# GpSimd copies two thirds of a shifted V tile, and the first column slot is kept in picture order

## The chip, the cores and the metric

The kernel runs on one core of a Trainium2 chip. A core has a matrix engine (TensorE, PE in the profile, with its weight loads as PEld), VectorE (DVE), ScalarE (ACT), GpSimd (POOL), and SyncE (SP), whose queue only issues transfers here. The metric is the device time of one launch in microseconds; lower is better.

## The reference, cut to what matters

The kernel computes neighborhood attention with 7x7 neighbours at a distance of 2 over a 224x224 picture of 192 channels:

```python
qkv = x @ wqkv                                  # x: (1, 224, 224, 192)
q, k, v = qkv[..., :C], qkv[..., C:2*C], qkv[..., 2*C:]
half = (7 - 1) // 2 * 2
r0 = clip(arange(H) - half, 0, H - 1 - 12)      # first row of the window
c0 = clip(arange(W) - half, 0, W - 1 - 12)      # first column of it
ri = r0[:, None] + arange(7) * 2
ci = c0[:, None] + arange(7) * 2
logits = einsum(q[n], k[rows ri, columns ci]) * C ** -0.5
o = einsum(softmax(logits), v[rows ri, columns ci]) @ wo
```

A pixel near the left edge has its window clipped to the start of the row. The pixels 0 to 5 of a row therefore look at the first window of even columns or at the first window of odd columns; on the right edge it is the same with the last windows.

## The kernel before

**Tiles.** With a distance of 2, a pixel only meets pixels of its own row and column parity. The kernel sorts the queries by the parity class of the rows (`rc`) and of the columns (`cc`) that they look at. The work goes in 14 steps: `steps` (L602) lists seven bands (`ti`) of 16 query rows, for both row classes. A step has 14 column slots of 8 query columns; slot 0 holds the clipped ones. A slot is a tile of 16 rows by 8 columns, 128 queries in all, once for each of the two column classes. Partitions 0 to 63 hold the first 8 rows and 64 to 127 the other 8.

**What is made for a step.** The input x is loaded transposed (L154, from SP) into XA and into a tile x1, of which GpSimd copies halves into XB (L160). GpSimd also sorts x by keys into XS (L170). From these TensorE makes two things.

- G is the query side with the key weights folded in: `g_items` (L395) multiplies x by AW. It works in four groups of slots, and each group is two whole tiles (`pg`, items g0 to g7) and one tile of halves (`pgh`, items h0 to h3). ACT evacuates them (L328); the halves go to a tile gx first, of which GpSimd copies each half into place (L450). `col_runs` (L378) says from which image columns the queries of a group come. It cuts them into runs that lie one behind the other in XA or XB; each run, for each run of rows, each half and both passes over the contraction, is one matmul at L415.
- V is the value side with wo folded in: `v_item` (L340), six matmuls (L335, L338) and one evacuation for each of 14 column blocks, items v0 to v13. The tile VV holds the values of the step. The second half of the queries reads it directly; the first half reads a tile in which the lower 64 partitions hold this step's values and the upper 64 those of the step before. `v_over` (L347) makes that tile: it copies partitions 0 to 63 from one VV tile to the other, in three pieces of column blocks. The pieces of the steps made in the background of steps 1 to 10 are blocks 0 to 4, 5 to 9 and 10 to 13, copied by DMAs that SP issues after items v4, v9 and v13 (L704 to L706). In the background of step 0 the pieces are 8, 3 and 3 blocks by DMAs that ACT (the first) and SP issue, and from the background of step 11 on they are 8, 3 and 3 blocks copied by GpSimd.

**What is done in a step.** A step is seven pairs of slots, and the loop at L714 runs over the 98 pairs. `stage1` multiplies G by x for the logits (L499) and takes the maximum with DVE (L501); `stage1b` takes the exponential with ACT (L508); `stage2` transposes the probabilities, by TensorE and a copy (L538, L539) or, for the pairs that TURN lists, by a DMA from SP (L522); `stage3` multiplies them by V (L548); `stage4` divides by the sum with DVE (L554, L571) and stores. stage3 runs two to three pairs behind stage1.

**Order.** All of it is written out by hand: the last call makes every engine run its instructions in program order. The items of the next step are mixed into the pairs by the tables BACK and LATE (steps 1 to 10, and later), with a lag of three pairs: item v9 is made in the first pair of the following step and v13 in its second, so the second and third piece of V's copy come there, and item h2 is made in the pair before them and h3 in the pair behind.

**Stores.** Slots 1 to 13 are stored by SP, in 96 KB for 16 rows, with a few short ones by GpSimd (L577). Slot 0 lies in another order: its columns are first three of one column parity and then those of the other, so that L597 lists five small stores for each run of rows in each half of a tile (L600). They are pushed into `pool_q` and issued by GpSimd, at most four items in a pair together with the sorts, which go ahead of them (L798, L804).

Of the kernel before, what the change touches and what calls it, by code (L numbers as in the profile page):

```python
# [19 lines left out]
S = 112  # L20
# [8 lines left out]
C = 192  # L29
# [38 lines left out]
def _win(t, p0, pn, off, dims):  # L68
    a = t[:]
    ps = a.ap[0][0]  # L70
    return bass.AP(a.tensor, a.offset + p0 * ps + off, [[ps, pn]] + [list(d) for d in dims])


def _x(par, v, c):

    return (v % RP) * RW + par * S + c
# [23 lines left out]
def kernel(  # L100
# [7 lines left out]
    nc = tc.nc  # L108
    B, H, W, C_ = x.shape
# [4 lines left out]
    op = out[0].rearrange("h (j two) c -> h j (two c)", two=2)  # L114
# [91 lines left out]
    for cc in range(2):  # L206
        t = pers.tile([128, S], BF, name=f"ch{cc}")
# [5 lines left out]
    d1 = setup.tile([128, MM], F32, name="d1")  # L213
# [133 lines left out]
    def v_over(rc, ti, c0, c1, eng=nc.sync.dma_start):  # L347

        eng(out=VV[rc][1 - ti % 2][0:64, c0:c1, :], in_=VV[rc][ti % 2][0:64, c0:c1, :])
# [26 lines left out]
        return runs  # L376

    def col_runs(cc, d0, d1):  # L378
        runs = []
        for d in range(d0, d1):  # L380
            if cc == 0:
                mem, pair = (1, d) if d < 3 else (0, d - 3)
            else:
                mem, pair = (1, 109 + d) if d < 3 else (0, 106 + d) if d < 6 else (1, d - 3)
            if runs and runs[-1][2] == mem and runs[-1][3] + runs[-1][1] == pair:
                runs[-1][1] += 1
            else:
                runs.append([d - d0, 1, mem, pair])
        return runs

    OUT_A = (0, 64)
# [3 lines left out]
    def g_items(rc, ti, s0, ns):  # L395
        rows = row_runs(rc, ti)
        w = 8 * ns

        def mm(pg, cc, p0, c0):

            out_ = []
            for (d0, dn, mem, pair) in col_runs(cc, 8 * s0, 8 * s0 + w):
                for (j, n, par, r) in rows:
                    o = _win(pg, p0, 64, j * w + d0, [[w, n], [1, dn]])
                    for pas in range(2):
                        X = (XA, XB)[pas][mem]
                        out_.append((o, AW[(mem, pas)][:, c0:c0 + 64], _win(X, 0, 128, _x(par, r, pair), [[RW, n], [1, dn]]), pas))
            return out_

        def both(a, b):  # L410
            for q in range(max(len(a), len(b))):
                for l_ in (a, b):
                    if q < len(l_):
                        (o, l, r, pas) = l_[q]
                        nc.tensor.matmul(o, lhsT=l, rhs=r, start=(pas == 0), stop=(pas == 1))  # L415

        def put(dst, off, pg, dve, p0=0, pn=128):

            a, m = s0, ns
            if s0 == 0:  # L420
                rr = [_runs8(rc, ti, h) for h in range(2)]
                if len(rr[0]) == len(rr[1]):
                    evac(_win(dst, p0, pn, off, [[64, 2], [8, 8], [1, 8]]), _win(pg, p0, pn, 0, [[8 * w, 2], [1, 8], [w, 8]]), dve)
                else:
                    for h in range(2):
                        for (j0, nj) in rr[h]:
                            evac(_win(dst, p0, pn, off + 64 * h + 8 * j0, [[nj, 8], [1, nj]]), _win(pg, p0, pn, (8 * h + j0) * w, [[1, 8], [w, nj]]), dve)
                a, m = 1, ns - 1
            evac(_win(dst, p0, pn, off + (a - s0) * 128, [[8, 16], [128, m], [1, 8]]), _win(pg, p0, pn, 8 * (a - s0), [[w, 16], [8, m], [1, 8]]), dve)

        def whole(cc):
            def emit(dve):
                pg = ps_g.tile([128, 512], F32, name="pg", tag="pg")
                both(mm(pg, cc, 0, OUT_A[cc]), mm(pg, cc, 64, OUT_A[cc] + 64))
                put(G[rc][cc], s0 * 128, pg, dve)
            return emit

        def halves(dve, direct=False):
            pg = ps_g.tile([128, 512], F32, name="pgh", tag="pg")
            pg1 = ps_o.tile([128, 512], F32, name="pgh", tag="o") if direct else pg  # L440
            both(mm(pg, 0, XDAT[0], OUT_B[0]), mm(pg1, 1, XDAT[1], OUT_B[1]))
            if direct:
                put(G[rc][0], (NSLOT + s0) * 128, pg, False, XDAT[0], 64)
                put(G[rc][1], (NSLOT + s0) * 128, pg1, True, XDAT[1], 64)
                return
            gx = work.tile([128, 512], BF, name="gx", tag="gx", bufs=3)
            put(gx, 0, pg, dve)
            for cc in range(2):
                p = XDAT[cc]
                nc.gpsimd.tensor_copy(out=G[rc][cc][p:p + 64, 1, s0:s0 + ns, :], in_=gx[p:p + 64, 0:ns * 128].rearrange("p (s q) -> p s q", q=128))  # L450

        return [whole(0), whole(1), halves]
# [104 lines left out]
    def stage4(J, ab):  # L557
        rc, ti, s, o_ps = J.rc, J.ti, 2 * J.m + ab, J.o_ps[ab]
        rs = J.rs.get(ab) or stage4a(J, ab)
        if s > 0 and J.n == NSTEP - 1:  # L560

            o_sb = _win(XS[0], 0, 128, 2 * C * s, [[C, 2], [1, C]])
        elif s > 0:
            o_sb = work.tile([128, 2, C], BF, name="o_sb", tag="o_sb", bufs=6)
        else:
            o_sb = work.tile([128, 2, C], BF, name="o_s0", tag="o_s0")
        if J.k >= NP - 3 and ab == 1:
            for cc in range(2):
                nc.scalar.mul(o_sb[:, cc, :], o_ps[:, 194 * cc:194 * cc + C], rs[:, cc:cc + 1])
        else:  # L570
            nc.vector.tensor_tensor(out=o_sb[:], in0=_win(o_ps, 0, 128, 0, [[194, 2], [1, C]]),  # L571
                                    in1=rs[:].unsqueeze(2).to_broadcast([128, 2, C]), op=ALU.mult)
        prow = _rows(rc, ti)
        if s > 0:
            for (j0, nj, r0, rstep) in _aff_runs(prow) if J.n < NSTEP - 1 else [(0, 12, prow[0], 2), (12, 1, prow[12], 1), (13, 3, prow[13], 2)]:
                def put(eng, j0=j0, nj=nj, r0=r0, rstep=rstep):
                    eng.dma_start(out=op[r0: r0 + (nj - 1) * rstep + 1: rstep, 8 * s - 3:8 * s + 5, :],  # L577
                                  in_=o_sb[8 * j0:8 * (j0 + nj)].rearrange("p t c -> p (t c)"))

                if J.n < NSTEP - 1:  # L580
                    put(nc.gpsimd if nj < 8 and s % 2 == 1 else nc.sync)
                elif nj >= 8:
                    put({NSLOT - 1: nc.scalar, NSLOT - 4: nc.gpsimd}.get(s, nc.sync))
                elif s in SHORT:

                    for j in range(nj):
                        def row(eng, p=8 * (j0 + j), r=r0 + j * rstep, a=SHORT[s]):
                            eng.dma_start(out=op[r, 8 * a - 3:8 * s + 5, :].rearrange("(t i) c -> i t c", i=8),
                                          in_=_win(XS[0], p, 8, 2 * C * a, [[2 * C, s + 1 - a], [1, 2 * C]]))
                        if s < NSLOT - 1:  # L590
                            row(nc.gpsimd)
                        else:
                            end_q.append(row)
            return
        for h in range(2):
            for (j0, nj, r0, rstep) in _aff_runs(prow[8 * h:8 * h + 8]):
                for (cc, i0, n, mem, pair) in ((0, 0, 3, 1, 0), (0, 3, 5, 0, 0), (1, 6, 2, 1, 3), (1, 0, 3, 1, 109), (1, 3, 3, 0, 109)):  # L597
                    p = 64 * h + 8 * j0 + i0 * nj
                    dst = op[r0: r0 + (nj - 1) * rstep + 1: rstep, pair:pair + n, mem * C:(mem + 1) * C]
                    pool_q.append(lambda dst=dst, p=p, m=n * nj, cc=cc: nc.gpsimd.dma_start(out=dst.rearrange("j i c -> i j c"), in_=o_sb[p:p + m, cc, :]))  # L600

    steps = [(ti, rc) for ti in range(7) for rc in range(2)]  # L602
    pairs = []
# [12 lines left out]
    act, dve, pool = nc.scalar.copy, nc.vector.tensor_copy, nc.gpsimd.tensor_copy  # L616
# [25 lines left out]
    pool_q = []  # L642
# [25 lines left out]
    t = ps_t.tile([128, 8, 128], BF, name="pt_ps", tag="pt")  # L668
# [33 lines left out]
    def back(it, by_dve):  # L702
        it(by_dve)
        for (i, c0, c1) in ((7, 0, 8), (10, 8, 11), (13, 11, 14)) if nb == 0 or nb >= 11 else ((4, 0, 5), (9, 5, 10), (13, 10, 14)):  # L704
            if it in vs and it is vs[i]:
                v_over(rcb, tib, c0, c1, pool if nb >= 11 else nc.sync.dma_start)  # L706

    def values_of(k):

# [4 lines left out]
    for k in range(NP + 2):  # L714
        J = pairs[k] if k < NP else None
        n = J.n if J else NSTEP
        w64, w128 = [], []
        if J:
            m = J.m
            nb, mb = divmod(k - LAG, 7)  # L720
            bg = k >= LAG and nb + 1 < NSTEP
            if bg and mb == 0:
                tib, rcb = steps[nb + 1]
# [115 lines left out]
```

## Time and profile before

| | before |
|---|---|
| median of 3 runs | 343.1 us (342.54 to 347.22) |
| the profiled execution's own time | 341.45 us |
| its span, first to last instruction | 339.7 us |
| TensorE busy | 322.4 us (95%), 7964 matmuls |
| VectorE busy | 311.0 us (92%) |
| ScalarE busy | 310.6 us (91%) |
| GpSimd busy | 288.2 us (85%) |
| packets on SP's DMA queue | 51.60 MB, 78.6% of 16 engines' span |
| small stores of slot 0 (L600) | 150, 84.5 us of GpSimd |
| SP's copies of V (L349) | 20 of 241.2 KB, 10 of 193.0 KB, 2 of 144.8 KB |

The busy times are for the whole span, and matmuls overlap, so a TensorE that is busy all the time is not yet one that is never held up. [...] A row of a group of instructions reads: line, engine, operation, what it writes and reads, shape of the output and the input, count, then busy time in us and mean ns of one, then the idle time of the engine ahead of them with what ended it. A wait that has several conditions is put down to the one that came last by the profile, which can be another than the one that decided.

### The profile page before, as it was taken

To read this page: it belongs to the slowest core of one execution; us is meant where nothing else is said; L and a number is where in the kernel's file an instruction comes from. 1 tells how busy PE (TensorE), PEld (TensorE's weight loads), DVE (VectorE), ACT (ScalarE), POOL (GpSimd) and SP (SyncE) were. 2 spreads that over 40 slices of the span, in tenths; PEclk is the share of its full clock that TensorE was granted. 3 is DMA by queue.
4 is the path that set the end of the run, shared out by engine and by line. 5 is a ranking of instruction groups with operands and counts; after the bars stand their busy time and mean duration, and the time that the engine had idled before them with its cause. 6 is when DMAs were issued, how large, how long until landed. Compare 5 with 4: busy or idle time off the path is not lost.

```text
span 339.7 us, 19155 instructions
## 1 busy us (share of the span) xinstructions
PE 322.4 (95%) x7964; PEld 296.2 (87%) x7964; DVE 311.0 (92%) x730; ACT 310.6 (91%) x816; POOL 288.2 (85%) x448
## 2 busy tenths in 40 slices
PE   4699999999999999999999999999999999999982
PEld 2578898898899999999999999998999999999871
DVE  8769999889999999999999999999999999999993
ACT  7779899999999999999999999999999999999982
POOL 8499999999979969789599597996987957999693
PEclk9999999999999999999999999999999999999998
DMA  8999655989979697697787988999989759668934
GB/s 189 213 159 201 130 117 123 213 193 191 172 182 184 146 214 151 136 194 159 173 183 147 197 166 138 208 152 168 195 131 210 173 134 134 128 133 157 150 83 100
DMA packets 135625, 55.43 MB, mean 163 GB/s; under 512 B 108729, under 2 KB 132754, under 8 KB 135539
## 3 DMA queue, kind: packets, MB, share of 16 engines
q1 hardware_dynamic: 129503, 51.60, 78.6%
q0 software_dynamic: 5376, 1.82, 3.0%
q8 instruction: 62, 1.02, 1.3%
q10 hardware_dynamic: 660, 0.80, 1.0%
q14 instruction: 24, 0.20, 0.2%
HBM read 0.29 MB, written 19.27 MB: 58 GB/s over the span
## 4 chain that ended last, share of the span: by engine, by line
PE 82%; ACT 7%; DVE 4%; SPq 3%; DMA 1%; issue 1%; DVEq 0%; ACTq 0%
PE s L499 18%; PE o_ps L548 17%; PE pg L415 13%; PE pv L335 10%; PE pv L338 8%; PE pt_ps L538 8%; PE pgh L415 7%; ACT p L508 4%; SPq L154 3%; DVE nmx L501 2%; DMA xa<-in_x_dram 1%; ACT v L328 1%; ACT gx L328 1%; ACT g L328 1%; DVE xs L571 1%
## 5 line engine op out<-in xcount | busy, mean ns | idle before, releaser
L508 ACT ACTIVATE p<-s,nmx 128x256 bf16<-128x256 f32 x392 | 163.0, 484 | 15.9 <-DVE nmx L501 14.0
L501 DVE TENSOR_REDUCE nmx<-s 128x2 f32<-128x448 f32 (+1 forms) x196 | 114.3, 624 | 10.8 <-PE s L499 5.7
L571 DVE TENSOR_TENSOR o_sb<-o_ps,rs 128x384 bf16<-128x384 f32 x169 | 94.2, 558 | 6.7 <-DMA out_dram<-o_sb 0.8
L499 PEld LDWEIGHTS <-g 128*64 128x64 bf16 x2592 | 86.8, 110 | 4.9 <-issue 1.2
L450 POOL COPY g<-gx 64x512 bf16<-64x512 bf16 (+1 forms) x110 | 61.7, 561 | 32.3 <-ACT gx L328 28.2
L328 ACT CAST v<-pv 128x384 bf16<-128x384 f32 x180 | 86.1, 515 | 3.2 <-PE pv L338 2.9
L600 POOL DMA_DIRECT2D out_dram<-o_s x150 | 84.5, 570 | 1.1 <-DVE rs L554 1.1
L499 PE MATMUL s<-xa,g 128*64 128x196 bf16 (+8 forms) x1296 | 83.1, 217 | 0.6 <-ACT p L508 0.4
L499 PE MATMUL s<-xb,g 128*64 128x196 bf16 (+8 forms) x1296 | 82.9, 217 | 0.2 <-ACT g L328 0.2
L548 PE MATMUL o_ps<-v,pt_sb 128*64 128x193 bf16 x1456 | 81.5, 246 | 1.1 <-DVE nmx L501 0.4
L335 PE MATMUL pv<-wb,xs 128*64 128x384 bf16 x406 | 74.3, 333 | 4.1 <-ACT xs L360 3.1
L338 PE MATMUL pv<-wp,xs 128*64 128x192 bf16 x812 | 74.8, 250 | 0.0
L548 PEld LDWEIGHTS <-pt_sb 128*64 128x64 bf16 x1456 | 66.4, 109 | 1.9 <-DVE xs L571 0.9
L338 PEld LDWEIGHTS <-xs 128*64 128x64 bf16 x812 | 60.5, 111 | 6.6
L415 PEld LDWEIGHTS <-aw 128*64 128x64 bf16 x1320 | 57.5, 111 | 6.2 <-issue 1.4
L328 ACT CAST g<-pg 128x512 bf16<-128x512 f32 (+4 forms) x139 | 60.5, 487 | 1.2 <-PE s L499 0.6
L415 PE MATMUL pg<-xb,aw 128*64 128x512 bf16 (+9 forms) x440 | 54.8, 269 | 0.0
L415 PE MATMUL pg<-xa,aw 128*64 128x512 bf16 (+9 forms) x440 | 53.4, 271 | 1.0 <-ACT gx L328 0.9
L538 PE MATMUL pt_ps<-ident,p 128*64 128x128 bf16 x1216 | 51.1, 219 | 0.0
L170 POOL COPY xs<-xa 128x896 bf16<-128x896 bf16 x51 | 46.5, 939 | 5.4 <-DMA xa<-in_x_dram 4.5
L539 DVE COPY pt_sb<-pt_ps 128x1024 bf16<-128x1024 bf16 x72 | 49.1, 682 | 0.4 <-PE pt_ps L538 0.3
L538 PEld LDWEIGHTS <-p 128*64 128x64 bf16 x1216 | 44.9, 110 | 0.5
(78 smaller groups left out, 336.4 us busy)
## 6 DMA issues: line engine op xcount, KB each, us to landing
out_dram<-o_sb SPq DMA_DIRECT2D x156, 96.0 KB
v<-v SPq DMA_DIRECT2D x20, 241.2 KB
v<-v SPq DMA_DIRECT2D x10, 193.0 KB
out_dram<-o_s POOLq DMA_DIRECT2D x78, 9.0 KB, 3.2
out_dram<-o_sb SPq DMA_DIRECT2D x13, 78.0 KB
xb<-xb SPq DMA_DIRECT2D x2, 448.0 KB
out_dram<-xs SPq DMA_DIRECT2D x11, 72.0 KB
v<-v SPq DMA_DIRECT2D x2, 337.8 KB
```

The costliest lines, as they stand in the source:

```text
L328: nc.scalar.copy(out=out_, in_=in_)
L335: nc.tensor.matmul(pv[64 * h:64 * h + 64, 0:2 * C], lhsT=at(1, h), rhs=WB[:].rearrange("p t c -> p (t c)"), start=True, stop=False, skip_g ...
L338: nc.tensor.matmul(pv[64 * h:64 * h + 64, cc * C:(cc + 1) * C], lhsT=at(2 * cc, h), rhs=WP[(cc, 0)], start=False, stop=True, skip_group_ch ...
L415: nc.tensor.matmul(o, lhsT=l, rhs=r, start=(pas == 0), stop=(pas == 1))
L450: nc.gpsimd.tensor_copy(out=G[rc][cc][p:p + 64, 1, s0:s0 + ns, :], in_=gx[p:p + 64, 0:ns * 128].rearrange("p (s q) -> p s q", q=128))
L499: nc.tensor.matmul(o, lhsT=w, rhs=r, start=(cc == 0 and done[h] == cols_), stop=(cc == 1 and not units[h]), skip_group_check=True)
L501: nc.vector.tensor_reduce(out=nmx[:], in_=_win(s_ps, 0, 128, lo, [[256, 2], [16, 16], [1, 16 - lo]]), axis=AX.XY, op=ALU.max, negate=True)
L508: nc.scalar.activation(out=J.p[:, ab, cc].rearrange("p q (r k) -> p q r k", k=8), in_=_win(s_ps, 0, 128, cc * 256, [[8, 2], [16, 16], [1, ...
L538: nc.tensor.transpose(pt_ps[64 * h:64 * h + 64, 4 * ab + 2 * cc + q, :], J.p[:, ab, cc, q, 64 * h:64 * h + 64], ident[:])
L548: nc.tensor.matmul(o_ps[64 * h:64 * h + 64, cc * 193:cc * 193 + 193], lhsT=J.pt[:, 4 * ab + 2 * cc + q, 64 * h:64 * h + 64], rhs=V[h][:, A ...
L571: nc.vector.tensor_tensor(out=o_sb[:], in0=_win(o_ps, 0, 128, 0, [[194, 2], [1, C]]), in1=rs[:].unsqueeze(2).to_broadcast([128, 2, C]), op ...
L600: pool_q.append(lambda dst=dst, p=p, m=n * nj, cc=cc: nc.gpsimd.dma_start(out=dst.rearrange("j i c -> i j c"), in_=o_sb[p:p + m, cc, :]))
```

## The change

There are three parts.

1. **V's copy.** In the background of steps 1 to 10 the second and third piece (after v9 and v13) are copied by GpSimd and no longer by a DMA from SP. The first piece stays with SP. The copies stand in GpSimd's order where the items are made, that is, ahead of that pair's sorts and stores and, of the items, behind h2 and ahead of h3.
2. **Slot 0 in picture order.** `col_runs` now interleaves the first six columns: three image columns of one parity go to columns 0, 2 and 4 of the tile and three of the other to 1, 3 and 5, so the matmul's output has a step of two elements there. Columns 6 and 7, and all later slots, are as before.
3. **Stores of slot 0.** For each run of rows there are three stores in place of five: six pixels of the left edge, six of the right edge, and two of both column classes that lie beside each other in memory.

```diff
     def col_runs(cc, d0, d1):
         runs = []
-        for d in range(d0, d1):
-            if cc == 0:
-                mem, pair = (1, d) if d < 3 else (0, d - 3)
-            else:
-                mem, pair = (1, 109 + d) if d < 3 else (0, 106 + d) if d < 6 else (1, d - 3)
-            if runs and runs[-1][2] == mem and runs[-1][3] + runs[-1][1] == pair:
+        if d0 == 0:
+            runs = [[0, 3, 2, 0, (S - 3) * cc], [1, 3, 2, 1, (S - 3) * cc]]
+        for d in range(6 if runs else d0, d1):
+            if runs and runs[-1][2:4] == [1, cc] and runs[-1][4] + runs[-1][1] == d - 3:
                 runs[-1][1] += 1
             else:
-                runs.append([d - d0, 1, mem, pair])
+                runs.append([d - d0, 1, 1, cc, d - 3])
         return runs
...
-            for (d0, dn, mem, pair) in col_runs(cc, 8 * s0, 8 * s0 + w):
+            for (d0, dn, dstep, mem, pair) in col_runs(cc, 8 * s0, 8 * s0 + w):
                 for (j, n, par, r) in rows:
-                    o = _win(pg, p0, 64, j * w + d0, [[w, n], [1, dn]])
+                    o = _win(pg, p0, 64, j * w + d0, [[w, n], [dstep, dn]])
...
-                for (cc, i0, n, mem, pair) in ((0, 0, 3, 1, 0), (0, 3, 5, 0, 0), (1, 6, 2, 1, 3), (1, 0, 3, 1, 109), (1, 3, 3, 0, 109)):
+                for (i0, n, cc0, c1, px, step) in ((0, 6, 0, 1, 0, 1), (0, 6, 1, 2, W - 6, 1), (6, 2, 0, 2, 6, 2)):
                     p = 64 * h + 8 * j0 + i0 * nj
-                    dst = op[r0: r0 + (nj - 1) * rstep + 1: rstep, pair:pair + n, mem * C:(mem + 1) * C]
-                    pool_q.append(lambda dst=dst, p=p, m=n * nj, cc=cc: nc.gpsimd.dma_start(out=dst.rearrange("j i c -> i j c"), in_=o_sb[p:p + m, cc, :]))
+                    dst = bass.AP(op.tensor, op.offset + r0 * W * C + px * C, [[step * C, n], [rstep * W * C, nj], [1, (c1 - cc0) * C]])
+                    pool_q.append(lambda dst=dst, src=o_sb[p:p + n * nj, cc0:c1, :]: nc.gpsimd.dma_start(out=dst, in_=src.rearrange("p t c -> p (t c)")))
...
-                v_over(rcb, tib, c0, c1, pool if nb >= 11 else nc.sync.dma_start)
+                v_over(rcb, tib, c0, c1, pool if nb >= 11 or nb > 0 and i in (9, 13) else nc.sync.dma_start)
```

## The prediction

> **What bounds the kernel now.** I read the page first, then the busy time of every engine step by step, then the waits.
>
> ```profile
> span 339.7 us, 19155 instructions
> PE 322.4 (95%) x7964; PEld 296.2 (87%) x7964; DVE 311.0 (92%) x730; ACT 310.6 (91%) x816; POOL 288.2 (85%) x448
> ...
> PE 82%; ACT 7%; DVE 4%; SPq 3%; DMA 1%; issue 1%; DVEq 0%; ACTq 0%
> ```
>
> All engines are nearly full, so the page alone doesn't decide. The chain that ended last lies on TensorE for 82% of the span. In the view of busy time by stretches I cut at the first reduction of each step; the rows below are steps 1 to 6 (stretch, its length, PE busy and its count, PEld, DVE, ACT, POOL, then granted clock, DMA share, GB/s).
>
> ```profile
> 46.41:69.16 22.75, 22.21 (x549) 19.90 (x546) 19.79 (x47) 21.52 (x58) 22.11 (x41) 1.00 0.78 161
> 69.16:91.78 22.62, 22.22 (x545) 20.49 (x542) 21.24 (x50) 21.61 (x58) 21.62 (x26) 1.00 1.03 192
> 91.78:113.81 22.03, 22.03 (x545) 20.67 (x542) 21.05 (x50) 21.20 (x57) 19.59 (x28) 1.00 0.83 176
> 113.81:136.25 22.44, 22.44 (x602) 21.08 (x599) 21.16 (x51) 21.25 (x57) 19.26 (x28) 1.00 0.84 173
> 136.25:159.11 22.86, 22.68 (x662) 21.09 (x658) 21.36 (x49) 21.28 (x57) 18.78 (x28) 1.00 0.80 166
> 159.11:181.17 22.06, 22.06 (x565) 21.14 (x562) 21.06 (x50) 21.21 (x57) 18.07 (x26) 1.00 0.80 166
> ```
>
> From step 3 on PE is busy for the whole stretch. The length follows the count of matmuls, and it does so although DVE, ACT and POOL do the same work: this is a TensorE bound, at full clock. Steps 1 and 2 are 0.72 and 0.59 us longer than step 3 with the same count, and there PE is idle for 0.54 and 0.40 us. The waits between 92 and 312 us say the same:
>
> ```profile
> POOL g L450 <- ACT gx L328: 27.3, 10, 3.5
> ACT p L508 <- DVE nmx L501: 8.5, 38, 0.3
> ...
> PE s L499 <- issue: 0.2, 1, 0.2
> ```
>
> The long wait is GpSimd's own, about once a step; ACT's are 0.2 us each, and PE's only one is 0.2 us. So for most of the span a gain on GpSimd, SP or the DMAs buys nothing, and a matmul more costs.
>
> **Part 2, the matmuls.** Each run of rows of a step's G takes six lists of matmuls for slot 0's group (two tiles with two halves, and the two of the half tile). For `cc` 0 the old `col_runs` gave two runs, 3 and 13 columns; the new one gives three: 3, 3 and 10. For `cc` 1 it stays at three. Three lists with one run more, two passes: six matmuls more per run of rows. Over the 14 steps there are 20 runs of rows, so 120 matmuls more, and no column more. What a cut costs is in the steps above, where bands that wrap around are cut in more pieces: 57 matmuls more cost 22.44 - 22.03 = 0.41 us (7.2 ns each), 117 cost 0.83 (7.1 ns), 20 cost 0.03 (1.5 ns). At 7.1 ns, 120 cost **+0.85 us**. Lower bound 120 x 1.5 = 0.2. For the upper bound I take a short matmul's whole place in a stream, in the timeline of PE (start, length, form, count):
>
> ```profile
> 195.85 0.19 PE L415 MATMUL pg<-xa,aw 128*64 128x48 bf16 x1
> ...
> 195.99 0.20 PE L415 MATMUL pg<-xb,aw 128*64 128x48 bf16 x1
> 196.02 0.25 PE L415 MATMUL pg<-xa,aw 128*64 128x160 bf16 x1
> ```
>
> Nine matmuls of 48 columns start in 0.17 us, 19 ns each: 2.3 us for 120. All of this is on PE's path; nothing hides it.
>
> The output of slot 0's six columns now steps by two elements. Of these stepped matmuls there are 24 per run of rows, 480 in all; before, no matmul wrote with such a step. I cost the step itself at nothing, by its nearest row, the 48-column matmuls above: they write runs of three and take 19 ns, though their columns alone would need less: a matmul of 193 columns takes 41 ns (the row at 79.25 below: 16 in 0.86 us, of which 0.25 is the last one's length), so 48 of them 10. From above I bound a stepped matmul by those 41 ns, as if each stepped column took four. That is 22 ns more each, 10.6 us for 480; it comes back as a rival. Evacuations keep their shapes: nothing.
>
> **Parts 1 and 3, GpSimd.** These are its groups:
>
> ```profile
> L600 POOL DMA_DIRECT2D out_dram<-o_s x150 | 84.5, 570 | 1.1 <-DVE rs L554 1.1
> L349 POOL COPY v<-v 64x3088 bf16<-64x3088 bf16 x2 | 5.5, 2754 | 0.1
> L349 POOL COPY v<-v 64x1158 bf16<-64x1158 bf16 x4 | 4.6, 1149 | 1.7 <-ACT v L328 1.7
> ```
>
> 150 stores at five per run are 30 runs; three per run are 90, so 60 x 0.57 = 34 us go. The new copies are 5 x 386 = 1930 and 4 x 386 = 1544 elements on 64 partitions. The two rows give (2754 - 1149) / (3088 - 1158) = 0.83 ns an element, so 1.79 and 1.47 us, 3.26 a step and 33 us in ten. GpSimd's sum hardly moves; per step it is 3.26 - 4 x 0.57 = +0.98 us, and what counts is where. At the start of step 9:
>
> ```profile
> 225.09 3.36 POOL L600 DMA_DIRECT2D out_dram<-o_s  x6
> 228.45 1.29 POOL L450 COPY g<-gx 64x512 bf16<-64x512 bf16 x2
> 229.68 1.69 POOL L600 DMA_DIRECT2D out_dram<-o_s  x3
> 234.37 1.28 POOL L450 COPY g<-gx 64x512 bf16<-64x512 bf16 x2 [3.00 <-ACT gx L328]
> ```
>
> Between h2's copies (228.45) and h3's (234.37) stand three stores and 3.00 us of idle time, 4.7 us in all. The stores are gone from there and the 3.26 us of copies go in: h3 starts when it did. Cost **0**, with that idle time as cover; without it, 0.98 us a step. Behind the copies wait h3, the next band's XB and sorts.
>
> On SP, 20 issues of about 0.55 us and 4.3 MB of transfers go. No wait of PE from step 3 on ends with them: **0**.
>
> **Steps 1 and 2** are where GpSimd and SP do reach PE. Step 1, from the timelines:
>
> ```profile
> 51.80 0.93 POOL L170 COPY xs<-x 128x896 bf16<-128x896 bf16 x1
> 52.76 1.43 SPq L154 DMA_TRANSPOSE x<-in_x_dram  x1
> 65.67 0.56 DVE L571 TENSOR_TENSOR o_sb<-o_ps,rs 128x384 bf16<-128x384 f32 x1 [0.83 <-DMA out_dram<-o_sb]
> 68.06 0.35 PE L335 MATMUL pv<-wb,xs 128*64 128x384 bf16 x2 [0.54 <-ACT v L328]
> ```
>
> SP's load waits for the sort that frees its tile (52.73), SP's stores stand behind it, DVE waits 0.83 us for a store's buffer, and through ACT it reaches PE as 0.54 us. Of the eleven slot-0 stores ahead of that sort two are gone (1.1 us), and SP is earlier by up to that. I take the whole stall out: **-0.5** (bounds -0.7, the step's excess, and 0). Late next is PE itself.
>
> Step 2 has the ten copies' worst place, since GpSimd has a backlog there:
>
> ```profile
> 68.97 0.63 ACT L328 CAST gx<-pgh 128x512 bf16<-128x512 f32 x1
> 71.10 1.13 POOL L600 DMA_DIRECT2D out_dram<-o_s  x2
> 72.22 1.29 POOL L450 COPY g<-gx 64x512 bf16<-64x512 bf16 x2
> 73.57 1.80 POOL L170 COPY xs<-xa 128x896 bf16<-128x896 bf16 x2
> 75.32 0.93 POOL L170 COPY xs<-x 128x896 bf16<-128x896 bf16 x1
> 76.20 3.41 POOL L160 COPY xb<-x 64x1792 bf16<-64x1792 bf16 x2
> 79.67 1.28 POOL L450 COPY g<-gx 64x512 bf16<-64x512 bf16 x2
> 78.60 0.25 PE L499 MATMUL s<-xb,g 128*64 128x84 bf16 x2
> 79.25 0.86 PE L548 MATMUL o_ps<-v,pt_sb 128*64 128x193 bf16 x16 [0.40 <-DVE nmx L501]
> 74.34 0.56 SPq L349 DMA_DIRECT2D v<-v  x1
> ```
>
> PE's o_ps at 79.25 needs V's second piece, issued at 74.34; that landing fits the wait better than the reduction the row names. In the new order the copy stands behind the XB copies that end at 79.61. With GpSimd no earlier than now it would end at 79.61 + 1.79 = 81.40, and PE would wait 2.2 us longer. But ten stores of steps 0 and 1 are gone, the two at 71.10 among them, so GpSimd arrives earlier, until h2's gx, evacuated at 69.60, holds it: 1.29 + 1.80 + 0.93 + 3.41 + 1.79 = 9.2 us later is 78.8. I take **-0.1** (bounds -0.4 and +2.2).
>
> **Sum:** 0.85 - 0.5 - 0.1 = +0.25 us. The profiled execution took 341.45 us, 1.75 more than its span, and becomes 341.7. The median of the runs, 343.1, lies 1.65 above it; I keep that distance: **343.3 us**. 2% (6.9 us) is about what a measurement of this kernel can tell from no change.
>
> **Rivals.**
>
> *Stepped output is slow* (slower). Each of the 480 stepped matmuls occupies PE for longer than the floor. At 41 ns in place of 19 it is +10.6, so 354. It decides from (6.9 - 0.25) / 480 = 14 ns more each, 33 ns. For it: no row shows a stepped write. Against: the floor of 19 ns leaves room before it shows. [...]
>
> *GpSimd comes late.* In step 2 the copy ends at 81.40 and PE waits: +2.2 in place of -0.1, so 345.6; with the cover lost in half of the ten steps (5 x 0.98) 350. Against: the idle time above.
>
> *All of SP's relief is felt.* Both excesses go (-0.72 - 0.59) and the matmuls cost 0.2: 342.0. To be 2% faster, 6.9 us would have to go, and PE has not so much to give between 46 and 312 us.
>
> *Copies hold up VectorE.* Beside GpSimd's copies (235.8 to 240 us, first pair of rows) and beside its stores (225.2 to 228.4, second pair):
>
> ```profile
> L539 DVE COPY pt_sb<-pt_ps 128x1024 bf16<-128x1024 bf16 x2 | 1.4, 680 | 0.0
> L571 DVE TENSOR_TENSOR o_sb<-o_ps,rs 128x384 bf16<-128x384 f32 x2 | 1.1, 558 | 0.1
> ...
> L571 DVE TENSOR_TENSOR o_sb<-o_ps,rs 128x384 bf16<-128x384 f32 x2 | 1.1, 558 | 0.1
> L539 DVE COPY pt_sb<-pt_ps 128x1024 bf16<-128x1024 bf16 x1 | 0.7, 681 | 0.0
> ```
>
> The same length and no idle time. Were each of the 20 copies to block DVE for half its length, 16 us would come on top, 359. [...]
>
> **How the numbers follow.** My forecast 0.60; GpSimd late, within 2%, 0.11, and beyond, 0.03; SP's relief 0.10; stepped output 0.11; VectorE held up 0.02; faster by over 2%, by something I don't see, 0.03. The range: the forecast's own terms reach from -0.7 - 0.4 + 0.2 = -0.9 to 2.2 + 2.3 = +4.5, so 342.2 to 347.6; downwards I drop the distance to the median, which may not hold (341.45 - 0.9): 340.5 to 347.6. Left out are stepped output, VectorE, GpSimd beyond 2% and the faster case: 0.19. Faster by over 2%: 0.03. Slower: 0.11 + 0.03 + 0.02 = 0.16. Within: 0.81.
>
> **What would show it.** Right: 8084 matmuls; step 3 at 22.08 us; 90 stores at L600 and L349 copies of 1.8 and 1.5 us; GpSimd's idle time ahead of h3 shrinks from 3.0 to between 1.4 and 2 us; no wait at 68 us. Wrong: stepped matmuls that start over 33 ns apart, PE waits on POOL in steps 2 to 11, DVE instructions longer than 558 and 681 ns.

## The result and the profile after

| | before | after |
|---|---|---|
| median, 13 runs each | 342.56 us (341.05 to 347.22) | 346.64 us (346.14 to 346.97) |
| the profiled execution's own time | 341.45 us | 346.83 us |
| its span | 339.7 us | 345.1 us |

The ratio of the times is 1.0117, with a 95% interval of 1.0096 to 1.0138: slower by 1.2%, inside the 2% that I had called the limit of what a measurement tells, and inside the range. But the runs resolve it well, and it is +4.1 us where I had forecast +0.25. That the range holds it is luck: its upper end was made up of a late copy in step 2 (2.2 us) and of dear cuts (2.3 us), and most of the 4.1 us come from a place that the sum doesn't have.

The page of the kernel after (span, engines, chain that ended last):

```profile
span 345.1 us, 19298 instructions
PE 323.8 (94%) x8084; PEld 301.9 (87%) x8084; DVE 311.2 (90%) x730; ACT 311.2 (90%) x816; POOL 288.4 (84%) x408
...
PE 80%; ACT 5%; DVE 3%; SPq 3%; POOL 3%; DMA 2%; issue 1%; DVEq 0%; ACTq 0%; POOLq 0%
```

TensorE has its 8084 matmuls and is busy for only 1.4 us more, though the span is 5.4 us longer. So most of what was lost lies where TensorE doesn't work. The view of busy time by stretches, cut as before at the first reduction of each step (steps 1, 2, 3 and 7: stretch, length, then PE, PEld, DVE, ACT, POOL busy, clock, DMA share, GB/s):

```profile
46.35:68.87 22.52, 22.40 (x555) 20.41 (x552) 19.95 (x46) 21.54 (x58) 19.63 (x36) 1.00 0.89 168
68.87:91.38 22.51, 22.40 (x552) 20.44 (x548) 21.21 (x49) 21.65 (x58) 21.30 (x23) 1.00 0.81 165
91.38:113.62 22.24, 22.24 (x551) 21.18 (x548) 21.08 (x50) 21.25 (x57) 21.51 (x27) 1.00 0.82 158
...
181.23:203.47 22.24, 22.24 (x551) 21.05 (x548) 21.08 (x51) 21.26 (x57) 19.74 (x25) 1.00 0.76 145
```

Steps 1 and 2 are 0.23 and 0.11 us shorter than before. Step 3 is 22.24 us where it was 22.03, and step 7 22.24 where it was 22.04: 0.20 us a step with TensorE busy throughout, for six matmuls more. From the first reduction to that of step 13 the two kernels differ by only 1.7 us. Of these, 0.66 lie in step 11 (22.07 us where it was 21.41), in which TensorE pauses for 0.4 us; five kernels below that have the new order too take 21.50 to 21.62 us for it. The rest is behind it: from the first reduction of step 13 to the end it took 27.46 us before and 31.30 us after, 3.84 us more.

That end is best read on the queues. The closing DRAIN of GpSimd's queue, before (the three numbers are the shortest, median and longest of three, in ns, then the first and last start):

```profile
L834 POOLq DRAIN  x3: 40/102/4960, 333.7 to 339.4; - x3
```

and after, in the same view:

```profile
L833 POOLq DRAIN  x3: 40/93/9035, 335.2 to 344.8; - x3
```

It begins in both kernels as GpSimd issues its last store, 0.3 us after the last matmul, and lasts 4.96 us before and 9.04 us after. Who waits for it is seen in SP's waits between 338 and 346 us of the kernel after:

```profile
SPq L833 <- PEq L833: 4.7, 2, 4.3
SPq L833 <- DMA out_dram<-xs: 1.0, 2, 0.6
```

SP has seen all its stores land by 340.2 us and then waits 4.3 us at the barrier that ends the program. The row names PE's queue, but PE had come to that barrier at 335.0, DVE at 335.8, ACT at 338.4; GpSimd came last, at 344.3, when its DRAIN was over. Before, GpSimd came at 338.65 and SP was last, at 338.9. So GpSimd's DRAIN costs the changed kernel 4.1 us (344.28 - 340.2), and cost the old one nothing. It isn't GpSimd's last store that it waits for: that landed at 337.3 us, 7.0 us before the DRAIN's end (before, 2.7 us ahead of it).

GpSimd in the steps did as forecast. Its groups after:

```profile
L599 POOL DMA_DIRECT2D out_dram<-o_s x90 | 51.1, 574 | 1.0 <-DVE rs L553 1.0
L349 POOL COPY v<-v 64x1930 bf16<-64x1930 bf16 x10 | 17.9, 1792 | 0.6
L349 POOL COPY v<-v 64x1544 bf16<-64x1544 bf16 x10 | 14.7, 1469 | 12.1 <-ACT v L328 12.1
```

and its timeline at the start of step 9:

```profile
225.39 2.82 POOL L599 DMA_DIRECT2D out_dram<-o_s  x5
228.21 1.30 POOL L449 COPY g<-gx 64x512 bf16<-64x512 bf16 x2
229.56 1.79 POOL L349 COPY v<-v 64x1930 bf16<-64x1930 bf16 x1
232.69 1.47 POOL L349 COPY v<-v 64x1544 bf16<-64x1544 bf16 x1 [1.33 <-ACT v L328]
234.73 1.28 POOL L449 COPY g<-gx 64x512 bf16<-64x512 bf16 x2 [0.58 <-PE pg L414]
```

h3's copies come 9.0 us after the step's first reduction (225.71), before it was 9.1. Of the 3.00 us of idle time 1.33 + 0.58 = 1.9 us are left.

What the stepped output did is seen in the groups of matmuls by form. The 48-column matmuls of whole tiles, before:

```profile
L415 PE MATMUL pg<-xb,aw 128*64 128x48 bf16 x48 | 4.4, 195 | 0.0
L415 PE MATMUL pg<-xa,aw 128*64 128x48 bf16 x48 | 4.3, 194 | 0.0
```

and after, all of them stepped:

```profile
L414 PE MATMUL pg<-xb,aw 128*64 128x48 bf16 x64 | 6.2, 220 | 0.0
L414 PE MATMUL pg<-xa,aw 128*64 128x48 bf16 x64 | 5.9, 213 | 0.0
```

One takes some 22 ns longer. Since matmuls overlap (in the prediction's rows they start 19 ns apart), this is not yet what the stream loses.

So there were two questions: what makes the DRAIN longer, and how the 0.20 us of a step divide between the cut, the step of two and the copies.

### The profile page after: what moved, and what is told of

Read it like the earlier page. It is cut to its first block, busy times and chain, and to the rows that moved or that the text cites. A ratio compares the mean times of both kernels' runs of the same rounds, so it can differ in the third digit from the quotient of the medians.

```text
span 345.1 us, 19298 instructions
## 1 busy us (share of the span) xinstructions
PE 323.8 (94%) x8084; PEld 301.9 (87%) x8084; DVE 311.2 (90%) x730; ACT 311.2 (90%) x816; POOL 288.4 (84%) x408
## 4 chain that ended last, share of the span: by engine, by line
PE 80%; ACT 5%; DVE 3%; SPq 3%; POOL 3%; DMA 2%; issue 1%; DVEq 0%; ACTq 0%; POOLq 0%
PE s L498 18%; PE o_ps L547 17%; PE pg L414 13%; PE pv L335 10%; PE pt_ps L537 8%; PE pv L338 8%; PE pgh L414 7%; ACT p L507 3%; SPq L154 3%; DVE nmx L500 2%; DMA xa<-in_x_dram 1%; POOL xb L160 1%; DMA out_dram<-o_sb 1%; POOL xs L170 1%; ACT g L328 1%
## 5 line engine op out<-in xcount | busy, mean ns | idle before, releaser
L498 PEld LDWEIGHTS <-g 128*64 128x64 bf16 x2592 | 88.1, 110 | 4.5 <-issue 1.5
L547 PE MATMUL o_ps<-v,pt_sb 128*64 128x193 bf16 x1456 | 82.7, 246 | 0.6 <-DVE xs L570 0.4
L335 PE MATMUL pv<-wb,xs 128*64 128x384 bf16 x406 | 75.9, 332 | 3.6 <-ACT xs L360 3.1
L338 PE MATMUL pv<-wp,xs 128*64 128x192 bf16 x812 | 76.2, 249 | 0.0
L414 PEld LDWEIGHTS <-aw 128*64 128x64 bf16 x1440 | 63.2, 112 | 5.8 <-issue 2.5
L338 PEld LDWEIGHTS <-xs 128*64 128x64 bf16 x812 | 63.6, 111 | 5.0
L414 PE MATMUL pg<-xa,aw 128*64 128x48 bf16 (+7 forms) x480 | 56.9, 267 | 1.9 <-ACT gx L328 0.9
L414 PE MATMUL pg<-xb,aw 128*64 128x48 bf16 (+8 forms) x480 | 58.1, 266 | 0.0
L349 POOL COPY v<-v 64x1930 bf16<-64x1930 bf16 (+3 forms) x26 | 42.6, 1643 | 15.0 <-ACT v L328 14.3
L599 POOL DMA_DIRECT2D out_dram<-o_s x90 | 51.1, 574 | 1.0 <-DVE rs L553 1.0
```

The lines of the kernel that those rows point to most:

```text
L335: nc.tensor.matmul(pv[64 * h:64 * h + 64, 0:2 * C], lhsT=at(1, h), rhs=WB[:].rearrange("p t c -> p (t c)"), start=True, stop=False, skip_g ...
L338: nc.tensor.matmul(pv[64 * h:64 * h + 64, cc * C:(cc + 1) * C], lhsT=at(2 * cc, h), rhs=WP[(cc, 0)], start=False, stop=True, skip_group_ch ...
L498: nc.tensor.matmul(o, lhsT=w, rhs=r, start=(cc == 0 and done[h] == cols_), stop=(cc == 1 and not units[h]), skip_group_check=True)
L547: nc.tensor.matmul(o_ps[64 * h:64 * h + 64, cc * 193:cc * 193 + 193], lhsT=J.pt[:, 4 * ab + 2 * cc + q, 64 * h:64 * h + 64], rhs=V[h][:, A ...
L599: pool_q.append(lambda dst=dst, src=o_sb[p:p + n * nj, cc0:c1, :]: nc.gpsimd.dma_start(out=dst, in_=src.rearrange("p t c -> p (t c)")))
```

## The experiments

The kernel before ran beside each group: 342.88 us in the first, 343.05 in the second, 343.28 in the third (medians of 10, 22 and 35 runs).

**The three parts taken apart.** First the copies alone, on the kernel before:

```diff
-                v_over(..., pool if nb >= 11 else nc.sync.dma_start)
+                v_over(..., pool if nb >= 11 or nb > 0 and i in (9, 13) else nc.sync.dma_start)
```

> Part 1 alone: GpSimd copies the second and third piece of V; slot order and five stores per run as before. After the result I hold two causes apart: slot 0's matmuls (steps 3, 7 and 8 went from 22.03 to 22.24 us) and the DRAIN that closes GpSimd's program (4.96 us before, 9.03 us in the changed kernel). The steps should be back at 22.03 here. If the longer DRAIN comes from having fewer GpSimd stores, it is 5.0 us here and the kernel is 0 to 0.5 us faster than before. If it comes from the copies, it is about 9 us here and the kernel is 3.5 to 4 us slower than before.

Measured: 346.95 us, ratio 1.0119 (1.009 to 1.0149). All of the loss lies in step 2; by stretches, steps 1 to 3 and then four pieces of step 2:

```profile
47.08:69.67 22.59, 22.23 (x549) 19.88 (x546) 19.78 (x46) 21.57 (x58) 21.90 (x42) 1.00 0.79 161
69.67:97.81 28.14, 24.92 (x545) 22.58 (x542) 21.35 (x49) 21.96 (x58) 27.45 (x31) 0.88 0.73 141
97.81:119.85 22.04, 22.04 (x545) 20.69 (x542) 21.01 (x51) 21.27 (x57) 20.95 (x28) 1.00 0.77 153
...
78.00:82.50 4.50, 1.36 (x30) 1.17 (x27) 2.15 (x5) 2.45 (x6) 4.38 (x4) 0.89 1.04 165
82.50:86.00 3.50, 3.43 (x50) 3.33 (x51) 1.12 (x3) 1.22 (x3) 3.38 (x5) 0.50 1.02 202
86.00:90.00 4.00, 4.00 (x77) 3.48 (x75) 2.59 (x7) 2.53 (x8) 3.85 (x4) 0.71 0.39 92
90.00:94.00 4.00, 4.00 (x102) 3.50 (x98) 3.89 (x11) 3.87 (x13) 3.81 (x6) 1.00 0.21 53
```

The DRAIN takes 4.87 us as before, so by the steps and the DRAIN it is the first reading; that the time is the second's is chance. From step 3 on the steps are those of before to within 0.13 us (step 5, in which the kernel before pauses, is 0.34 shorter): the copies cost nothing there. In step 2 GpSimd comes late. Its timeline, and then TensorE's:

```profile
72.14 1.13 POOL L600 DMA_DIRECT2D out_dram<-o_s  x2
73.27 1.30 POOL L450 COPY g<-gx 64x512 bf16<-64x512 bf16 x2
74.63 1.81 POOL L170 COPY xs<-xa 128x896 bf16<-128x896 bf16 x2
76.38 0.93 POOL L170 COPY xs<-x 128x896 bf16<-128x896 bf16 x1
77.26 3.41 POOL L160 COPY xb<-x 64x1792 bf16<-64x1792 bf16 x2
80.73 3.21 POOL L349 COPY v<-v 64x1930 bf16<-64x1930 bf16 x2
...
82.57 1.50 PE L548 MATMUL o_ps<-v,pt_sb 128*64 128x193 bf16 x16 [3.22 <-POOL v L349]
```

The first copy stands behind the XB copies, as in my rival, starts at 80.73 and ends 1.8 us later; TensorE waits 3.2 us for it. And with the wait comes something that I hadn't in the sum: the granted clock falls, and TensorE is busy for 24.92 us with the work of 22.22. By the rows above the mean clock is 0.89 from 78.0 to 82.5 us, 0.50 in the 3.5 us behind that, 0.71 in the next 4 and 1.00 from 90 us on. The step is 5.5 us longer: TensorE is idle for 3.2 us where it was for 0.4, and busy for 2.7 us more. The wait ends at 82.57 us, so the clock had begun to fall before it was over.

With five stores per run of rows the copies cost this much; the prediction's step 2 (copies and stores together) held because ten stores were gone ahead of them. To see whether the rest of the ten steps is free, the copies of step 2 were left on SP:

```diff
-nb > 0 and i in (9, 13)
+nb > 1 and i in (9, 13)
```

> The kernel before, with the copies on GpSimd in the steps after step 2 alone (the two copies that fall into step 2 stay on SP; order of slot 0 and its five stores unchanged). Copies on GpSimd from step 2 on took 346.95 us against 342.88, with step 2 at 28.14 us in place of 22.62 and the later steps as before. If that loss is step 2's queue on GpSimd alone, step 2 is back at 22.6 us, the later steps are at 22.04, the DRAIN ends 4.25 us after the last issue, and the time is 342.5 to 343.3. If the copies cost anywhere else, 344 or more.

Measured: 343.76 us, ratio 1.0009 (0.9984 to 1.0034). Step 2 is 22.06 us. So the loss of 4 us was step 2's. In steps 9 and 10 TensorE waits 0.1 us for a copy, and step 9 is 0.2 us longer than before; waits of 1.0 us in step 1 and 0.7 in step 3, for other things, hide what else a copy may cost or gain.

Then the other two parts without the copies (`pool if nb >= 11 else nc.sync.dma_start`, on the kernel after):

> Parts 2 and 3 alone: picture order and three stores per run; SP copies all of V as before. Steps 3, 7 and 8 at 22.24 us by either reading. DRAIN: 9 us if fewer stores make it long (then 5.5 to 6 us slower than before), 5 us if the copies make it long (then about 2 us slower).

Measured: 349.35 us, ratio 1.0191 (1.0156 to 1.0227), 2.7 us more than with the copies. The steady steps are 22.23 to 22.27 us, the DRAIN is 9.03 us as in the changed kernel. TensorE's waits from step 1 to 12 are not:

```profile
PE o_ps L547 <- DMA pt_x<-p: 1.3, 1, 1.3
PE o_ps L547 <- DMA pt_sb<-p: 1.0, 1, 1.0
PE pt_ps L537 <- issue: 1.0, 1, 1.0
```

Two of the three are for transposes by DMA, which SP issues as it issues V's pieces. In the changed kernel the same view holds one row, 0.4 us of "issue". So with the new order the kernel is faster with the copies than without (the intervals of the two ratios don't meet), though with the old one no gain showed. That SP's copies held up these transposes is only argued. In step 2 the copies cost something all the same: it takes 22.23 us here, without them, and 22.51 in the changed kernel.

Next the cut without the step: the kernel before with the 13 columns of `cc` 0 cut into 3 and 10, 120 matmuls more, and no stepped output:

```diff
-if runs and runs[-1][2] == mem and runs[-1][3] + runs[-1][1] == pair:
+if runs and runs[-1][2] == mem and runs[-1][3] + runs[-1][1] == pair and (cc, d) != (0, 6):
```

> Before, with the run of 13 columns cut into 3 and 10: the same 120 matmuls more as in the changed kernel, but no stepped output; stores and copies as before. If the step of two in the output costs the time, step 7 is 22.07 us (six matmuls at 7 ns) and the mean of a 48-column matmul stays at 195 ns. If the number of matmuls costs it, step 7 is 22.24 us. Whole kernel 0.8 us slower than before by the first, 2.2 us by the second. DRAIN as before, 5 us.

Measured: 346.2 us, ratio 1.0086 (1.0053 to 1.0119). The whole time is spoiled by pauses of 0.1 to 1.4 us in steps 2, 4, 5 and 6; the undisturbed steps tell what was asked. Step 8 before, with the cut, and in the changed kernel:

```profile
203.21:225.24 22.03, 22.03 (x545) 20.68 (x542) 21.06 (x50) 21.20 (x57) 19.59 (x29) 1.00 0.89 166
207.45:229.56 22.11, 22.11 (x551) 20.91 (x548) 21.09 (x50) 21.26 (x57) 18.66 (x27) 1.00 0.85 175
203.47:225.71 22.24, 22.24 (x551) 21.21 (x548) 21.09 (x51) 21.26 (x57) 19.75 (x25) 1.00 0.71 147
```

Taken over steps 3, 7 and 8 it is 22.04 before, 22.11 with the cut, 22.24 with cut and step; and 22.24 as well in the kernel with the new order that has SP's copies and five stores (below), so neither copies nor stores make the difference. Six matmuls more cost 0.07 us, 12 ns each; 24 stepped ones 0.13 us, 5.4 ns each. The 48-column matmuls take 195 to 199 ns here, and 213 to 220 in both kernels with the step.

**The DRAIN.** The three kernels above already bear on it: with 162 GpSimd DMAs (copies alone, cut alone) the DRAIN takes 4.87 us and ends 4.25 us after GpSimd's last issue, as before; with 102 (order and stores without copies) it takes 9.03 us and ends 8.41 us after it, as in the changed kernel. So the copies have no part in it. The next one keeps the new order but splits the six-pixel stores in two, which makes it 162 again (copies on SP):

```diff
-((0, 6, 0, 1, 0, 1), (0, 6, 1, 2, W - 6, 1), (6, 2, 0, 2, 6, 2))
+((0, 3, 0, 1, 0, 1), (3, 3, 0, 1, 3, 1), (0, 3, 1, 2, W - 6, 1), (3, 3, 1, 2, W - 3, 1), (6, 2, 0, 2, 6, 2))
```

> Picture order with the stores of six pixels cut in two, so again five per run and 150 in all; SP copies all of V. Step 7 at 22.24 us. DRAIN: 5 us if the number of stores sets it, whatever their shape; 9 us if picture order or the shape sets it. Whole kernel about 2 us slower than before by the first, 6 us by the second.

Measured: 347.4 us, ratio 1.0147 (1.0118 to 1.0177), and TensorE again pauses in the steps. The DRAIN ends 4.25 us after the last issue:

```profile
L833 POOLq DRAIN  x3: 40/93/4868, 339.9 to 345.5; - x3
```

It is the number of GpSimd's DMAs, then, or the number near the end, and neither the order nor the shape. Two more kernels split the stores in the last two steps only (112 DMAs) and in the first seven only (132), on the kernel after:

> The changed kernel, but in the last two steps slot 0's six-pixel stores are split in two, five per run of rows: 112 GpSimd DMAs in place of 102. If the stores near the end decide how long GpSimd's closing DRAIN takes, it ends 4.25 us after GpSimd's last issue, as with 162 DMAs, and the time falls by about 4 us less one or two for ten more issues at the end: 343 to 344.5 us. If the count over the whole program decides, 112 is nearer to 102: the DRAIN ends 8.4 us after the last issue, and the time stays at 346.5 to 347.5.

> The changed kernel, but in steps 0 to 6 slot 0's six-pixel stores are split in two: 132 GpSimd DMAs, with the last seven steps as in the changed kernel. If the stores near the end decide the DRAIN: 8.4 us after the last issue, 346.5 us or, with GpSimd later in step 2, up to 349. If the count over the whole program decides, 132 lies halfway between 102 (8.41 us) and 162 (4.25 us): a gradual dependence gives some 6.3 us, a threshold gives one of the two values; at 4.25 the span is 4 us shorter, and the time 342.5 to 345 by what step 2 loses.

Measured: 348.45 us (1.0152, 1.0099 to 1.0205) and 347.24 us (1.0107, 1.0072 to 1.0141). With 112 the DRAIN became longer still; the row of it in the kernel with the split at the end:

```profile
L833 POOLq DRAIN  x3: 40/93/9852, 337.2 to 347.6; - x3
```

With 132 it lasted 3.04 us, shorter than ever and less than either reading had, though its last seven steps were those of the changed kernel. The end's stores don't decide. That kernel's time shows nothing of this because ten more stores in steps 0 and 1 made GpSimd late in step 2: TensorE waited 2.8 us for the copy, the clock was 0.67 in the mean of the 4 us behind it, and the step took 26.75 us.

The five values that I had then (one, 152, from a kernel that is told of below) fell on one line if the count was taken modulo 128, and I bet on that: 132 stores with the split in the late steps, where it hurts nobody, and the same with six stores fewer, 126.

```diff
+... in (five if J.n >= 7 else three)         # 132 DMAs
+... in (five if 7 <= J.n < 13 else three)    # 126 DMAs
```

> The changed kernel, with slot 0's six-pixel stores split in two from step 7 on: 132 GpSimd DMAs, the first seven steps as in the changed kernel. So far GpSimd's closing DRAIN ended 2.42 us (132 DMAs), 3.59 (152), 4.25 (162), 8.41 (102) and 9.23 (112) after its last issue: all five lie near 2.2 us + 0.061 us x (DMAs modulo 128). If the count modulo 128 decides, it ends about 2.4 us after the last issue, steps 1 to 12 keep the changed kernel's lengths, SP is last at the end, and the time is 342.3 to 343.5 us: the changed kernel less its 4.1 us of waiting for GpSimd. If something in the early steps' stores brought the 2.42, it stays at 8.4 or more and the time at 346.6.

> As the version with 132 DMAs, but the last step keeps its three stores per run of rows: 126 GpSimd DMAs, six fewer. By the count modulo 128 the DRAIN ends 2.2 + 126 x 0.061 = 9.9 us after the last issue, and the time is that of the changed kernel plus some 1.5 us, 347.5 to 348.5. If the dependence were one of fewer DMAs making it longer, it would end near the 132's 2.4 to 3 us, and the time would be 342.5 to 343.5.

Measured: 344.96 us (1.0043, 1.0018 to 1.0068) and 343.3 us (0.9999, 0.9975 to 1.0023). The second one refutes the exact form of the rule: 126 DMAs gave the shortest DRAIN of all, 2.15 us after the last issue in place of 9.9.

```profile
L833 POOLq DRAIN  x3: 40/93/2775, 335.8 to 341.2; - x3
```

With 132 in the late steps it ended 3.79 us after the last issue; there the last step's own additional stores put GpSimd's last issue off to 338.9 us. All that was measured:

| GpSimd DMAs | kernels | DRAIN's length | its end after GpSimd's last issue |
|---|---|---|---|
| 102 | after; order and stores | 9.04, 9.03 us | 8.41, 8.41 us |
| 112 | five at the end | 9.85 us | 9.23 us |
| 126 | five late, not in the last step | 2.78 us | 2.15 us |
| 132 | five early; five late | 3.04; 5.03 us | 2.42; 3.79 us |
| 152 | three kernels with the new order in steps 0 and 1 | 4.22, 4.22, 4.29 us | 3.59, 3.59, 3.59 us |
| 162 | before; copies alone; cut alone; order, five stores | 4.96, 4.87, 4.87, 4.87 us | 4.25 us in all four |

Shown is that the DRAIN's length changed with the number of GpSimd's DMAs in these kernels, and that those with 102, 152 or 162 agree to within 0.1 us. By the ends after the last issue, with the 2.42 us for 132, it is about 0.06 to 0.08 us more for each further DMA from 102 to 112 and from 132 on, and between 112 and 126 it drops by some 7 us. What makes the slope and the drop is not shown, nor why the two kernels with 132 differ by 1.4 us, and no run tells where in 113 to 126 the drop lies.

What the DRAIN costs the change is shown by the pair: the changed kernel with 24 more small stores in steps 7 to 12 is level with before, 3.3 us faster than without them by the medians (by the two ratios 1.2%, which is 4.0 us), and its steps 1 to 10 are those of the changed kernel to within 0.02 us.

**A version that beats both?** The stores' relief is wanted in steps 1 and 2, and the new order costs some 0.2 us in nearly every step; so I kept new order and three stores in steps 0 and 1 alone (152 DMAs), with all ten steps' copies, with those of step 2 alone, and with none:

```diff
-for (d0, dn, dstep, mem, pair) in col_runs(cc, 8 * s0, 8 * s0 + w):
+for (d0, dn, dstep, mem, pair) in col_runs(cc, 8 * s0, 8 * s0 + w, 2 * ti + rc >= 2):   # True: the old runs
```

> The changed kernel with slot 0's new order and its three stores in steps 0 and 1 alone, the old order and five stores from step 2 on; the copies on GpSimd in all ten steps (152 GpSimd DMAs). If the new order costs 0.2 us a step by its cut and its step of two, if step 2 needs only that GpSimd comes to it sooner, and if the DRAIN goes by the number of DMAs: step 1 at 22.5 to 22.7, step 2 at 22.3 to 22.6, steps 3 on at 22.04 like before, DRAIN 4.25 us after the last issue; 342.2 to 342.8 us, level with before or 0.3 us under it. If step 2's copies need the shorter stores of step 2 itself, step 2 is over 24 us and the time 344.5 to 347.

> Slot 0's new order and three stores in steps 0 and 1 alone, and of the copies only step 2's two on GpSimd; the rest as before (152 GpSimd DMAs). From the steps measured so far: 0.43 us off step 1 and 0.31 off step 2, steps 3 on as before (22.04, 22.43, ...), the end as before: 342.3 us, 0.7 under before (ratio 0.998), which is less than this comparison can show; step lengths show it. If the later copies were of use in the version with all ten, this one has steps over 22.04 in steps 3 to 10 and is at 343 or more.

> The same with no copy on GpSimd in steps 1 to 10: only slot 0's new order and three stores in steps 0 and 1. If step 2's gain is the copies', step 2 is back at 22.6 to 22.8 us with PE waiting some 0.6 us for V at its start, step 1 stays at 22.3, and the time is 342.6 us. If it is GpSimd's shorter queue, step 2 stays at 22.3.

Measured: 342.73 us (0.9987, 0.9962 to 1.0012), 343.28 us (0.9991, 0.9965 to 1.0016) and 342.64 us (0.9985, 0.9958 to 1.0013). None is faster than before by more than its interval. The last one's steps 1, 2 and 5:

```profile
47.07:69.38 22.31, 22.19 (x549) 19.91 (x546) 19.86 (x47) 21.49 (x58) 19.55 (x36) 1.00 0.80 170
69.38:91.41 22.03, 22.03 (x545) 20.67 (x542) 21.06 (x49) 21.49 (x58) 16.84 (x19) 1.00 0.90 184
...
135.87:159.92 24.05, 22.82 (x662) 21.48 (x657) 21.16 (x50) 21.31 (x57) 17.62 (x26) 1.00 0.92 158
```

Step 1 lost 0.44 us and step 2 the whole of its excess: without copies on GpSimd it takes 22.03 us, with them 22.31. So what helps there is GpSimd's shorter queue, and the copies cost 0.28 us of it. With all ten steps' copies and five stores, steps 3 and 4 took 22.35 and 22.79 us, some 0.3 more than before, where the copy came 0.3 us late: that is the "cover lost" of my rival, at a third of its price. With the same five stores, copies alone lost nothing in these steps. The version with step 2's copies alone has steps 5 and 7 at 24.64 and 22.69 us and is over 343; by what I had put down, that speaks for the later copies.

What took the last one's gain back is in the third row: step 5 was 24.05 us, 1.5 more than in the undisturbed profiles (22.53), with one pause of 1.2 us of kind "issue". Such a pause stands in step 5 of several kernels, 0.2 us (before), 1.0 (order and stores), 2.0 (order, five stores). The timeline of the last of these:

```profile
152.82 0.50 PE L537 MATMUL pt_ps<-ident,p 128*64 128x128 bf16 x11
155.31 0.33 PE L537 MATMUL pt_ps<-ident,p 128*64 128x128 bf16 x5 [2.00 <-issue]
```

It stands in the middle of 16 transposes for which the profile shows no wait ("issue"). Step 5 has the most matmuls of all, 662 to 675 in about the time of 545 to 551. What TensorE waits for there is not shown. One DMA queue (q8, marked "instruction") brings packets of 16 KB, 62 of them before and 63 in the changed kernel, in which TensorE has 7964 and 8084 matmuls and as many weight loads. The pause of the kernel before ends at 152.49 us, 1.4 us after such a packet, and the one of 0.4 us in step 11 of the changed kernel at 284.70 us, 1.5 us after one; two pauses don't show that the packets have to do with them. The four kernels named here with a pause in step 5 (0.2, 1.0, 1.2 and 2.0 us) have SP copy all of V for that step. The changed kernel and the one with all ten steps' copies and the new order in steps 0 and 1 alone have GpSimd copy two pieces, and no pause of at least 0.2 us there.

## Why the prediction was right and wrong

**What bounds the kernel.** Right: from step 3 on length followed TensorE's work, and GpSimd's, SP's and the DMAs' gains bought nothing in those steps. But the argument stopped at step 12. What ends the program was never looked at, and there lies most of the loss.

**120 more matmuls at 7.1 ns, +0.85.** The count was right. The size was not: 12 ns each in an undisturbed step, within my bounds of 1.5 and 19 ns. That price came from steps where bands wrap around, a cut of another kind; and the 0.83 us that I read for 117 matmuls held a pause, since step 5 takes 22.53 us where it is undisturbed, which makes it 4.3 ns each.

**The step of two at nothing.** Wrong by a little that adds up: 5.4 ns for each of the 480 matmuls, about 0.13 us a step. This was the rival "stepped output is slow", with the sign right and its price of 22 ns four times too high. In the rows a 48-column matmul goes from 195 to 213 and 220 ns; in the stream it is 5 ns more, where the prediction read 19 from start to start. Together the two terms come to some 2.3 us, summed over the undisturbed steps (0.20 us in most, 0.23 in steps 4 and 10, 0.1 in steps 0, 11 and 12), where I had 0.85. That is the first mis-sized term, and step 3, which I had put at 22.08 us as a sign of being right, was 22.24.

**GpSimd's copies at nothing.** Right in steps 3 to 11: h3 starts as before and 1.9 us of idle time remain, as said. My reason, the cover, is borne out in part: with five stores kept, steps 3 and 4 grew by 0.3 us in one kernel, but not with the copies alone. Wrong in step 2, where they cost 0.28 us. VectorE was not held up; its instructions take 557 and 681 ns in the changed kernel, as before.

**SP's relief at nothing.** No gain showed against the old order: with copies from step 3 on the ratio is 1.0009 (0.9984 to 1.0034). It was not the whole story. With the new order and the copies on SP the kernel was 2.7 us slower than with the copies on GpSimd, and TensorE waited in its profile for two DMA transposes (2.3 us) and for nothing that the profile shows (1.0 us). That SP's traffic is what delays them is argued, not shown.

**Step 1, -0.5.** The stall at 68 us shrank. TensorE's idle time there went from 0.54 to 0.12 us (67.66 to 67.78 in its timeline); of the 0.4 us that this gave, 0.2 went into the dearer matmuls, and the step was 0.23 shorter. "No wait at 68 us" was nearly so.

**Step 2, -0.1.** The number is right, -0.11, but it is a net of things that I hadn't apart: GpSimd's shorter queue took away the whole excess of 0.59 us, the dearer matmuls cost 0.2 and the copies 0.28. The copy started at 76.8 us, not at 79.6, and ended at 78.6; the matmul that needs it began at 78.68, some 0.3 us late. So TensorE did wait for GpSimd, one of my signs of being wrong, if for little. That it hung on the stores that had gone was right: with the five stores kept, it was my rival "GpSimd comes late" that came true. That rival was priced at 2.2 us and measured 5.5, 2.8 by waiting and 2.7 because the clock fell as well (0.50 in the mean of the 3.5 us behind the wait).

**The term that wasn't there: GpSimd's closing DRAIN.** The sum took the 60 stores fewer as a gain or as nothing. They were a loss: 102 GpSimd DMAs in place of 162 made the closing DRAIN 4.08 us longer, and all of it was at the end of everything. Before, GpSimd came to the closing barrier only 0.25 us ahead of SP (338.65 and 338.9), so there was no cover; I could have read that, and looked at neither. That a shorter list would make it longer I couldn't have read from one trace.

**The distance to the median.** I kept 1.65 us; it was 1.1 before (13 runs) and -0.2 after. The profile of before was a favourable run of a kernel whose runs range over 6 us; those of after lie within 0.8 us. This hides some 1.3 us of the change: the profiles differ by 5.4 us, the medians by 4.1. Nothing here settles why before's runs scatter and after's don't; the pauses in step 5 (0.2 us in before's profile, none in that of the changed kernel) may have a part in it.

## What to carry to other kernels

Follow the last microseconds of the program engine by engine, and see who comes to the closing barrier last and by how much: an engine that is off the critical path in every step can still be the one that ends the run. Price a cheap instruction by the stream it stands in, times the number of steps: 0.2 us a step is no more than the smallest wait that I listed, and the 2.3 us that it comes to are more than the change saved in steps 1 and 2. And here waits on TensorE of 2.8 and 3.2 us cost 1.6 and 1.8 times their length, since the clock fell (to 0.67 in the mean of the 4 us behind the first, to 0.50 in that of the 3.5 us behind the second).

## What was not expected of the hardware

- GpSimd's closing DRAIN changed with the number of DMAs that GpSimd had issued in the program: it ended 2.15 us after the last issue with 126, 4.25 with 162, 8.41 with 102, 9.23 with 112. The 60 fewer of the changed kernel made it 4.1 us longer.
- When TensorE waited 3.2 us, the granted clock was 0.89 in the mean of the 4.5 us up to the wait's end, 0.50 in the 3.5 us behind it and 0.71 in the 4 us behind those; with a wait of 2.8 us it was 0.67 in the mean of the next 4 us.
- A matmul output with a step of two fp32 elements took 213 to 220 ns in place of 195 for 48 columns, and 5.4 ns more of the stream.
- TensorE paused for 0.2 to 2.0 us between two matmuls where the profile shows no wait: 0.2 us before, 0.4 in the changed kernel, 1.0 (order and stores), 1.2 (new order in steps 0 and 1, no copies) and 2.0 (order, five stores).
